# Requesting the MLP's weights in slices and reordering the opening of an attention-plus-MLP kernel

## The chip, the core and the metric

The kernel runs on one core of a Trainium2 chip. The metric is the device time of one execution in microseconds. PE is TensorE, ACT ScalarE, DVE VectorE, POOL GpSimd and SP SyncE, which here issues nearly all DMAs.

## What is computed

```
xn  = layernorm(x)                                    # x: 2048 x 640
q, k, v = split(xn @ wqkv)                            # 32 heads of 20
att = softmax(q @ k^T / sqrt(20)) @ v                 # per head
y   = layernorm(xn)
h   = gelu(y @ w1 + b1)                               # 640 -> 1536
out = x + att @ wo + (h @ w2 + b2)                    # 1536 -> 640
```

Inputs and the output are float32.

## The kernel before

The products are done in float16 pairs: a float32 number is scaled by a power of two and split into a high and a low half, and three products (high x high, high x low, low x high) stand for one. The power of two of each weight is found on the chip. ACT squares the weight and sums along the row (`Square` with `accum_out`), which gives a column per slice in a tile `acc`. `pow2` (L102) adds up the partitions with a product of `ones` and `acc` on PE (L111), adds up the columns on DVE (L112) and makes the power of two in five small DVE steps. `scale_of` (L416) calls it and leaves the scale `s_q`, `s_k` or `s_v` and, for q and k, the factor `qks`.

The program's first part runs over four chunks of 512 rows. Its order on each engine is the order in which it is written. For a chunk, rows are normalized (`norm_a` takes statistics and the root, `norm_b` refines it by a Newton step on DVE and scales the rows, `norm_c` refines the second layernorm's factor and stores it to `rscr`, a transfer of 512 pieces of four bytes), turned (`transp`, or in chunk 0 the transposes at L502 and L504) into `xnt`, and stored to `xscr` for the MLP. Then come five tiles `tt` of q and k: `qk` (30 products), `qk_out` (ACT makes the high half, DVE the low half in the buffer `hl`, of which there are two; two DMAs store it to `qkscr`), and `qk_sq` (squares for the lengths of the heads). Then come four tiles of v (`vproj`, `vproj_out`).

Chunk 0 is the opening. `load_x(0)` and the five slices of wqkv's q part are requested first, then its k part. `load_x(1)` reuses the tiles of x's first block and so waits for the transposes that read them; wqkv's v part, `xscr`, `bscr`, `b1t` and `rscr` follow in the same SP queue, and behind them the stores of the first q/k tile. `warm` issues products without a use, 37 at the start and 5 ahead of the first real ones. The tile `mxp` of `pow2` and the tile `pt4` of the fifth column of transposes share one PSUM buffer (`psM`), so that the transposes to `pt4` begin when DVE has read `mxp`. The q, k and v parts of wqkv are kept, until they are split, in the space of the MLP's weights: q and v in `w1t`, k in `w2t`.

The MLP's weights W1 (640 x 1536) and W2 (1536 x 640) are requested in chunk 0, each by one DMA: W2 behind tile 1 (L540), W1 in tile 4 (L548). `weights()` (L456) is a generator of small steps: six squares of W2 (two of its twelve row blocks each), its scale, five squares of W1 (a row block each), its scale, and then the splits. `some(n)` takes n of its steps, from the v tiles of chunk 0 on.

After chunk 3 the attention begins, with the MLP's and the output's products filled in between; the change doesn't touch that part.

Each DMA of SP's queue also waits until the DMA eight before it has landed, because the DMAs use eight semaphores in turn.

Of the kernel before, what the change touches and what calls it, by code (L numbers as in the profile page):

```python
# [7 lines left out]
F32 = mybir.dt.float32  # L8
# [3 lines left out]
AF = mybir.ActivationFunctionType  # L12
ALU = mybir.AluOpType
AX = mybir.AxisListType
PSUM = bass.MemoryType.PSUM
DRAM = bass.MemoryType.DRAM
P = 128
# [25 lines left out]
def mha_mlp_kernel(tc, x, wqkv, wo, w1, b1, w2, b2, out):  # L43
# [4 lines left out]
    with (  # L48
# [53 lines left out]
        def pow2(acc, tag):  # L102

            lo = keep.tile([P, 1], F32, name=f"lo_{tag}")
            hi = keep.tile([P, 1], F32, name=f"hi_{tag}")
            if tag in ("q", "k"):
                pt = psM.tile([P, 512], F32, tag="m", name="mxp")
            else:
                pt = psS.tile([P, 2, 512], F32, tag="s", name="mxp")[:, 0, :]
            n = acc.shape[1]  # L110
            nc.tensor.matmul(pt[:, :n], ones, acc, start=True, stop=True)  # L111
            nc.vector.tensor_reduce(lo, pt[:, :n], AX.X, ALU.add)  # L112
            nc.vector.tensor_scalar(lo, lo, 2.0**-100, 2.0**120, ALU.max, ALU.min)

            nc.vector.tensor_scalar(lo.bitcast(I32), lo.bitcast(I32), 0x7F000000, 1,
                                    ALU.bitwise_and, ALU.logical_shift_right)
            nc.vector.tensor_scalar(lo, lo, 2.0**64, None, ALU.mult)
            exponents(lo, hi)
            return lo, hi
# [42 lines left out]
        with tc.tile_pool(name="pa", bufs=2) as pa, tc.tile_pool(name="pa1", bufs=1) as pa1, tc.manual_schedule():  # L162
# [65 lines left out]
                nc.vector.tensor_scalar(t, t, -0.5 * by, 1.5 * by, ALU.mult, ALU.add)  # L228
                nc.vector.tensor_mul(dst, dst, t)

            def norm_a(c):

                xt = xts[c]
                st = pa.tile([P, 4, 2, 6], F32, tag="st", name="st")
                mv = pa.tile([P, 4, 2], F32, tag="mv", name="mv")
                ve = pa.tile([P, 4], F32, tag="ve", name="ve")
                r = pa.tile([P, 4], F32, tag="r", name="r")
                r2 = pa.tile([P, 4], F32, tag="r2", name="r2")
                for j in range(4):
                    for i in range(2):  # L240
                        nc.vector.bn_stats(st[:, j, i, :], xt[j][:, i * 320 : (i + 1) * 320])
                    nc.vector.bn_aggr(mv[:, j, :], st[:, j])
                nc.vector.tensor_scalar(ve, mv[:, :, 1], EPS, None, ALU.add)
                if c == 0:
                    nc.scalar.activation(r, ve, AF.Sqrt)
                    nc.vector.reciprocal(r, r)
                else:
                    nc.gpsimd.tensor_tensor(r, ve, nhalf, ALU.pow)
                rs[c] = mv, ve, r, r2
# [164 lines left out]
            def sums(tag, ws):  # L414
                accs[tag] = squares(ws, junk)
# [40 lines left out]
            def weights():  # L456

                for i in range(KF // 2):
                    if i == 0:
                        accs["2"] = sm.tile([P, 8], F32, tag="acc2", name="acc2", bufs=1)[:, : KF // 2]  # L460
                    nc.scalar.activation(junk[:, : 2 * D].rearrange("p (a b) -> p a b", a=2),
                                         w2t[:, 2 * i : 2 * i + 2, :], AF.Square, accum_out=accs["2"][:, i : i + 1])
                    yield
                scale_of("2")
                yield
                for k in range(KD):
                    if k == 0:
                        accs["1"] = sm.tile([P, 8], F32, tag="acc1", name="acc1", bufs=1)[:, :KD]
                    nc.scalar.activation(junk[:, :F], w1t[:, k, :], AF.Square, accum_out=accs["1"][:, k : k + 1])
                    yield  # L470
                scale_of("1")
                yield
                factors()
                yield
                for k in range(KF):
                    split(pa, w2t[:, k, :], w2v[:, k, 0], w2v[:, k, 1], scales["2"], D)
                    yield
                for k in range(KD):
                    for q in range(3):
                        split(pa, w1t[:, k, q * 512 : (q + 1) * 512], w1v[:, k, q, 0], w1v[:, k, q, 1], scales["1"], 512)  # L480
                        yield

            slices = weights()

            def some(n):
# [2 lines left out]


            warm(37)  # L490
            norm_a(0)
            sums("q", [stage["q"][:, k] for k in range(KD)])
            norm_b(0)
            xnts[0] = pa.tile([P, KD, 2, 512], F16, tag="xnt", name="xnt0")
            pts = [psS.tile([P, 2, 512], F32, tag="s", name="pt") for _ in range(2)]
            pt = [pts[0][:, 0], pts[0][:, 1], pts[1][:, 0], pts[1][:, 1]]
            for j in range(4):
                if j == 3:
                    scale_of("q")
                    pt.append(psM.tile([P, 512], F32, tag="m", name="pt4"))  # L500
                for k in range(KD - 1):
                    nc.tensor.transpose(pt[k][:, j * P : (j + 1) * P], xts[0][j][:, k * P : (k + 1) * P], ident)  # L502
            for j in range(4):
                nc.tensor.transpose(pt[4][:, j * P : (j + 1) * P], xts[0][j][:, 4 * P :], ident)  # L504
            warm(5)

            for k in range(KD):
                nc.scalar.activation(xnts[0][:, k, 0, :], pt[k], AF.Copy)
# [6 lines left out]
            for c in range(4):  # L515
                nxt = c + 1 if c < 3 else None
                for tt in range(5):
                    if c == 0 and tt == 1:
                        norm_b2(0)
                        norm_c(0)  # L520

                        nc.scalar.activation(junk[:, :1], ones[:, :1], AF.Exp)
                        ps = qk(0, 1, lambda: scale_of("k"))
                        hl = qk_out(0, 0, first)
                        split_qkv("q", c0=4 * P)
                        split_qkv("k")
                    else:
                        ps = qk(c, tt)
                    if tt == 3:
                        lengths(4)  # L530

                    if c == 0:
                        if tt == 0:
                            split_qkv("q", c0=2 * P, c1=4 * P)
                            sums("k", [stage["k"][:, 0:3], stage["k"][:, 3:]])
                            first = ps
                            continue
                        elif tt == 1:
                            qk_sq(0, 0, hl)
                            nc.sync.dma_start(w2t, w2.rearrange("(k p) n -> p k n", p=P))  # L540
                        elif tt == 2:
                            sums("v", [stage["v"][:, 0:3], stage["v"][:, 3:]])
                            norm_a(1)
                        elif tt == 3:
                            scale_of("v")
                            split_qkv("v")
                        elif tt == 4:
                            nc.sync.dma_start(w1t, w1.rearrange("(k p) n -> p k n", p=P))  # L548
                    else:

                        step = tt - (c == 1)
                        if nxt and 0 <= step < 3:
                            (norm_a, norm_b, norm_c)[step](nxt)
                            some(1)
                        else:
                            some(2)
                    qk_out(c, tt, ps)
                    if nxt and c > 0 and tt >= 2:
                        for j in ((0,), (1, 2), (3,))[tt - 2]:
                            turn(nxt, j)  # L560
                    if c == 3 and tt == 2:
                        early = [load_features(mc) for mc in range(2)]
                if c == 1:
                    load_x(3)
                if c == 3:
                    stack = load_stack(0, 0)
                    for _ in range(6):
                        next(stack)
                for j in range(4):
                    ps = vproj(c, j)  # L570
                    if j == (0 if c == 3 else 1):
                        lengths(10)
                    if c == 0:
                        if j < 2:
                            (norm_b, norm_c)[j](1)

                        pts = []
                        for k in ((), (0,), (2, 4), ())[j]:
                            transp(1, k, pts)
                        for t in pts:  # L580
                            transp_out(*t)
                    if j == 0 and c == 3:
                        shifts()
                        for _ in stack:
                            pass
                    some(2 if c < 3 else 1)
                    vproj_out(c, j, ps)
                if c == 0:
                    load_x(2)
            some(99)  # L590
# [630 lines left out]
```

## Time and profile before

| | us |
|---|---|
| median of 3 runs | 1363.1 (1362.19 to 1364.39) |
| profiled execution, its time | 1364.71 |
| its span | 1363.0 |
| PE busy in the span | 1335.1 (98%) |
| ACT busy | 1129.6 (83%) |
| DVE busy | 1060.5 (78%) |
| granted clock, mean | 0.998 |

Times in the views are counted from the start of the profiled execution's span; its time is 1.7 us more than its span. A row of a timeline has the start, the length, the engine, the line, the operation, what is written and read, and in brackets how long the engine was idle before it and who ended that.

### The profile page before, as it was taken

What the parts mean: (1) busy time and instruction counts of PE and PEld (TensorE: products, weight loads), DVE (VectorE), ACT (ScalarE), POOL (GpSimd) and SP (SyncE); (2) the same over time, 40 slices, a digit from 0 to 9 for tenths busy, and PEclk for the clock granted to TensorE, in tenths of its full rate; (3) what the DMA queues carried; (4) which work ended last, traced back from release to release, by engine and by line L of the source; (5) the groups of instructions that cost most, each with busy time, mean ns of one, the idle gap of its engine ahead of it and who ended that gap; (6) DMA issues with size and microseconds to landing.
All of it is one profiled execution on the core that took longest, in us unless ns stands there. A gap on an engine that the chain in (4) does not pass through costs nothing.

```text
span 1363.0 us, 29029 instructions
## 1 busy us (share of the span) xinstructions
PE 1335.1 (98%) x11651; PEld 591.6 (43%) x11651; DVE 1060.5 (78%) x1436; ACT 1129.6 (83%) x1305; POOL 30.2 (2%) x74
## 2 busy tenths in 40 slices
PE   9999999999999999999999999999999999999998
PEld 6545545443334334433433343434433333333465
DVE  6658835998779897978797789897879898888732
ACT  6654525999999999999999999999999999999700
POOL 2000000000000000000000000000000000000000
PEclk9999999999999999999999999999999999999999
DMA  9868731111113221212321141223032223244275
GB/s 269 270 157 154 146 101 57 34 52 43 48 58 94 62 83 60 52 50 84 93 71 51 37 109 48 86 62 86 19 87 85 70 81 86 59 135 118 88 233 175
DMA packets 103073, 127.94 MB, mean 94 GB/s; under 512 B 27516, under 2 KB 69568, under 8 KB 102932
## 3 DMA queue, kind: packets, MB, share of 16 engines
q1 hardware_dynamic: 99864, 119.60, 31.2%
q0 software_dynamic: 2304, 5.24, 2.4%
q8 instruction: 93, 1.52, 0.5%
q10 hardware_dynamic: 764, 1.18, 0.3%
q14 instruction: 48, 0.39, 0.1%
HBM read 80.50 MB, written 42.51 MB: 90 GB/s over the span
## 4 chain that ended last, share of the span: by engine, by line
PE 79%; DVE 9%; ACT 7%; issue 3%; DMA 2%; ACTq 0%; SPq 0%; DVEq 0%
PE o L711 26%; PE s L680 17%; PE py L945 11%; PE pu L913 9%; PE qkp L322 8%; PE vp L395 5%; ACT p L682 4%; PE z L1024 4%; DVE low L694 3%; DMA oa<-ev 1%; DVE u L849 1%; DMA qkscr<-qkhl 1%; DVE u L850 1%; DVE w L853 1%; DVE w L854 1%
## 5 line engine op out<-in xcount | busy, mean ns | idle before, releaser
L682 ACT ACTIVATE p<-s 128x1024 f32<-128x1024 f32 x1024 | 972.3, 1041 | 43.4 <-PE s L680 37.0
L694 DVE TENSOR_TENSOR low<-p 128x1024 f16<-128x1024 f32 x512 | 610.7, 1219 | 159.9 <-ACT p L682 159.7
L711 PE MATMUL o<-p,vfull 128*32 128x512 bf16 (+1 forms) x4096 | 430.8, 493 | 0.0
L680 PE MATMUL s<-qs,ks 61*128 61x512 f16 x2048 | 316.5, 382 | 7.4 <-ACT p L682 6.5
L680 PEld LDWEIGHTS <-ks 61*128 61x128 f16 x2048 | 63.7, 94 | 293.6 <-issue 291.3
L913 PE MATMUL pu<-xm,w1t 128*128 128x256 f16 x1440 | 179.3, 274 | 1.4 <-DVE u L849 1.4
L945 PE MATMUL py<-w2t,hT 128*128 128x320 f16 x1152 | 178.5, 300 | 1.5 <-DVE u L849 1.5
L913 PEld LDWEIGHTS <-w1t 128*128 128x128 f16 x1440 | 130.5, 98 | 68.8 <-issue 55.1
L945 PEld LDWEIGHTS <-hT 128*128 128x128 f16 x1152 | 102.4, 98 | 88.6 <-issue 54.3
L322 PE MATMUL qkp<-xnt,wv 128*128 128x512 f16 x600 | 132.7, 383 | 2.3 <-DVE qkhl L338 2.1
L711 PEld LDWEIGHTS <-vfull 128*32 128x32 f16 x3072 | 60.8, 95 | 139.8 <-issue 108.5
L711 PE MATMUL o<-low,vfull 128*32 128x512 f16 x1024 | 104.0, 378 | 4.3 <-DVE low L694 4.3
L322 PEld LDWEIGHTS <-wv 128*128 128x128 f16 x600 | 58.7, 99 | 73.2 <-issue 2.6
L711 PEld LDWEIGHTS o<-p,vfull 128*32 128x32 f32 x2048 | 62.6, 108 | 51.3
L337 ACT ACTIVATE qkhl<-qkp,qks 128x1024 f16<-128x1024 f32 (+1 forms) x24 | 23.2, 968 | 66.5 <-PE qkp L322 43.3
L1024 PE MATMUL z<-w1t,ot 128*128 128x320 f16 x480 | 66.7, 300 | 1.8 <-DVE oa L837 1.8
L395 PE MATMUL vp<-wv,xnt 128*128 128x320 f16 x480 | 66.7, 299 | 0.0
L338 DVE SCALAR_TENSOR_TENSOR qkhl<-qkp,qks,qkhl 128x1024 f16<-128x1024 f32 (+1 forms) x24 | 26.5, 1105 | 45.3 <-ACT qkhl L337 44.5
L1024 PEld LDWEIGHTS <-ot 128*128 128x128 f16 x480 | 46.3, 98 | 23.1 <-issue 2.9
L395 PEld LDWEIGHTS <-xnt 128*128 128x128 f16 x480 | 46.7, 98 | 18.7
L983 DVE SCALAR_TENSOR_TENSOR acc<-z,sc,acc 128x320 f32<-128x320 f32 x32 | 17.5, 550 | 43.2 <-PE z L1024 39.9
L732 ACT ACTIVATE ev<-o 128x512 f32<-128x512 f32 x64 | 39.2, 612 | 4.2 <-PE o L711 4.1
(179 smaller groups left out, 666.7 us busy)
## 6 DMA issues: line engine op xcount, KB each, us to landing
qkscr<-qkhl SPq DMA_DIRECT2D x40, 256.0 KB
opart<-ev SPq DMA_DIRECT2D x124, 80.0 KB
ks<-qkscr SPq DMA_DIRECT2D x120, 80.0 KB
qs<-qkscr SPq DMA_DIRECT2D x192, 40.0 KB
oa<-opart SPq DMA_DIRECT2D x32, 240.0 KB
xt<-in_A_x_dram SPq DMA_DIRECT2D x16, 320.0 KB
xscr<-xnt SPq DMA_DIRECT2D x4, 1280.0 KB
xm<-xscr SPq DMA_DIRECT2D x8, 640.0 KB
```

What stands on the lines that cost most here:

```text
L322: nc.tensor.matmul(ps[:, i, :], wv[:, k, q, a, mm * P : (mm + 1) * P], xnts[c][:, k, b, :], start=(k + n == 0), stop=(k == KD - 1 and n == 2))
L337: nc.scalar.activation(hl[:, 0, i0:i1], ps[:, i0:i1], AF.Copy, scale=a)
L338: nc.vector.scalar_tensor_tensor(hl[:, 1, i0:i1], ps[:, i0:i1], a, hl[:, 0, i0:i1], ALU.mult, ALU.subtract)
L395: nc.tensor.matmul(ps[:, hf, :320], xnts[c][:, k, a, j * P : (j + 1) * P], wv[:, k, 2, b, hf * 320 : (hf + 1) * 320], start=(n == 0), stop ...
L680: nc.tensor.matmul(ps[:, a, :], ks[64 * a : 64 * a + 61, kb * P : (kb + 1) * P], qs[64 * a : 64 * a + 61, cc * 512 : (cc + 1) * 512], star ...
L682: nc.scalar.activation(pt, ps, AF.Exp, scale=QS)
L694: nc.vector.tensor_sub(low, pt, upper(pt))
L711: nc.tensor.matmul(pv.o[32 * q : 32 * q + 32, :], src[:, v0 - PAD * (1 - q % 2) :][:, :32], t, start=q not in pv.begun, stop=last, skip_gr ...
L732: nc.scalar.activation(evs[g, hf][:, cc], pv.o, AF.Copy)
L913: nc.tensor.matmul(ps[:, i], w1v[:, k, (f + i) // 4, a, fo_ : fo_ + P], xnt[:, k, b, :], start=(n == 0), stop=(n == 3 * KD - 1))
L945: nc.tensor.matmul(ps[:, :320], hTs[mc][:, f, a, j * P : (j + 1) * P], w2v[:, f, b, hf * 320 : (hf + 1) * 320], start=(n == 0), stop=(n == ...
L1024: nc.tensor.matmul(ps[:, :320], ot[:, k, a, j * P : (j + 1) * P], wov[:, k, b, h * 320 : (h + 1) * 320], start=(n == 0), stop=(n == 3 * KD ...
```

## The change

The two DMAs for the MLP's weights become eleven: six for W2 (two row blocks each), five for W1 (one row block each). A generator `requests()` issues them, and `ask(n)` takes n: 1, 2, 2 and 1 behind `qk_out` of tiles 1 to 4 of chunk 0, then 2, 1, 1 and 1 behind its four v tiles.

In the opening, the square of q's first slice stands ahead of the `Sqrt` on ACT, the other four behind it. All sixteen transposes to the first four columns come ahead of `scale_of("q")`, where the last four stood behind it. The columns of `acc` are added up in PSUM, by one product for each column, and DVE's reduction is left out; this holds wherever `pow2` is called. Three products without use instead of five stand ahead of the first real ones.

```diff
             n = acc.shape[1]
-            nc.tensor.matmul(pt[:, :n], ones, acc, start=True, stop=True)
-            nc.vector.tensor_reduce(lo, pt[:, :n], AX.X, ALU.add)
-            nc.vector.tensor_scalar(lo, lo, 2.0**-100, 2.0**120, ALU.max, ALU.min)
+            for i in range(n):
+                nc.tensor.matmul(pt[:, :1], ones, acc[:, i : i + 1], start=(i == 0), stop=(i == n - 1))
+            nc.vector.tensor_scalar(lo, pt[:, :1], 2.0**-100, 2.0**120, ALU.max, ALU.min)
...
-            def norm_a(c):
+            def norm_a(c, between=None):
...
                 if c == 0:
+                    between()
                     nc.scalar.activation(r, ve, AF.Sqrt)
...
+            def requests():
+
+                for i in range(KF // 2):
+                    nc.sync.dma_start(w2t[:, 2 * i : 2 * i + 2], w2r[:, 2 * i : 2 * i + 2])
+                    yield
+                for k in range(KD):
+                    nc.sync.dma_start(w1t[:, k], w1r[:, k])
+                    yield
+
+            w2r, w1r = (w.rearrange("(k p) n -> p k n", p=P) for w in (w2, w1))
+            asked = requests()
+
+            def ask(n):
+                for _ in range(n):
+                    next(asked, None)
...
             warm(37)
-            norm_a(0)
-            sums("q", [stage["q"][:, k] for k in range(KD)])
+            accs["q"] = sm.tile([P, 8], F32, tag="acc", name="acc")[:, :KD]
+
+            def square_q(ks):
+                for k in ks:
+                    nc.scalar.activation(junk[:, :D], stage["q"][:, k], AF.Square, accum_out=accs["q"][:, k : k + 1])
+
+            norm_a(0, lambda: square_q((0,)))
+            square_q(range(1, KD))
             norm_b(0)
...
             for j in range(4):
-                if j == 3:
-                    scale_of("q")
-                    pt.append(psM.tile([P, 512], F32, tag="m", name="pt4"))
                 for k in range(KD - 1):
                     nc.tensor.transpose(pt[k][:, j * P : (j + 1) * P], xts[0][j][:, k * P : (k + 1) * P], ident)
+            scale_of("q")
+            pt.append(psM.tile([P, 512], F32, tag="m", name="pt4"))
             for j in range(4):
                 nc.tensor.transpose(pt[4][:, j * P : (j + 1) * P], xts[0][j][:, 4 * P :], ident)
-            warm(5)
+            warm(3)
...
                         elif tt == 1:
                             qk_sq(0, 0, hl)
-                            nc.sync.dma_start(w2t, w2.rearrange("(k p) n -> p k n", p=P))
...
-                        elif tt == 4:
-                            nc.sync.dma_start(w1t, w1.rearrange("(k p) n -> p k n", p=P))
...
                     qk_out(c, tt, ps)
+
+                    ask((0, 1, 2, 2, 1)[tt] if c == 0 else 0)
...
                     vproj_out(c, j, ps)
+                    if c == 0:
+                        ask(2 if j == 0 else 1)
```

## The prediction

> **What bounds the kernel now.** I read the page first. PE is busy 98% of the span and the chain of waits is 79% PE, so only time that PE loses counts. Of the groups of instructions, none that the change touches is large; all of it lies before 80 us. There I read the timeline engine by engine. PE, whole rows, then what holds it:
>
> ```profile
> 11.75 1.61 PE L502 MATMUL pt<-ident,xt 128*128 128x128 f32 x12 [0.17 <-DVE xt L255]
> 14.17 0.39 PE L111 MATMUL mxp<-acc,ones 128*128 128x5 f32 x2 [0.81 <-ACT junk L95]
> 14.41 0.63 PE L502 MATMUL pt<-ident,xt 128*128 128x128 f32 x4
> 14.88 0.60 PE L504 MATMUL pt<-ident,xt 128*128 128x128 f32 x4
> 15.32 1.28 PE L220 MATMUL warm<-ones 128*128 128x128 f32 x10
> 16.43 10.53 PE L322 MATMUL qkp<-xnt,wv 128*128 128x512 f16 x48
> ...
> 42.95 0.38 PE L111 MATMUL mxp<-acc,ones 128*128 128x2 f32 x2
> 45.47 8.34 PE L322 MATMUL qkp<-xnt,wv 128*128 128x512 f16 x30 [2.14 <-DVE qkhl L338]
> ```
>
> Each row is start, length, engine, line; the bracket is idle time before it. Real products begin at 16.43. From there PE stops once, for 2.14 us before 45.47, and otherwise runs on past 220 us (its only other gap there is 0.20 us at 73.21). So there are two prices: when 16.43 comes, and the stall at 43.33.
>
> The chain of waits names the stall's cause, and the busy time by stretch shows what surrounds it (columns: stretch, length, PE, PEld, DVE, ACT, POOL busy, clock, DMA share, GB/s):
>
> ```profile
> 31.22 10.78 DMA qkscr<-qkhl
> 42.00 0.02 issue
> 42.02 0.04 ACTq L337
> 42.06 0.38 issue
> 42.44 0.69 ACT qkhl L337
> ```
> ```profile
> 32.50:38.00 5.50, 5.50 (x28) 2.46 (x26) 5.04 (x10) 5.47 (x6) 0.00 (x0) 1.00 0.87 19
> 42.80:46.20 3.40, 1.26 (x22) 0.72 (x11) 2.15 (x7) 2.07 (x3) 0.00 (x0) 1.00 1.00 375
> 46.20:49.60 3.40, 3.40 (x10) 1.21 (x9) 2.47 (x5) 3.14 (x5) 0.00 (x0) 0.50 1.03 403
> 1305.70:1309.10 3.40, 1.61 (x13) 0.94 (x12) 2.67 (x3) 0.00 (x0) 0.00 (x0) 1.00 0.02 8
> ```
>
> The copy-out of the third q/k tile (tt 2) reuses the first tile's buffer, and must wait for that tile's two stores, 256 KB each, which take 10.78 us. From 32.5 to 38 the DMA engines are 87% busy and move 19 GB/s: this follows `rscr`'s store of 512 four-byte pieces, and the same collapse follows the next `rscr` stores at 73 and 106 us. W2's 3.84 MB is requested at 34.99, behind these stores, and its packets start only at 38.85, when the collapse is over. So the stall is `rscr`'s doing, not W2's. After the stall the clock is 0.50 for 3.4 us; the 30 matmuls take 8.34 instead of 30 x 0.215 = 6.45 us, some 1.8 us more.
>
> The opening's ACT rows, and the one table load with work on both sides:
>
> ```profile
> 9.75 0.21 ACT L245 ACTIVATE r<-ve 128x4 f32<-128x4 f32 x1 [7.64 <-DVE ve L243]
> 9.86 0.72 ACT L95 ACTIVATE junk<-w1t 128x640 bf16<-128x640 f32 x1
> 10.48 0.19 ACT L95 ACTIVATION_READ_ACCUMULATOR junk<-w1t 128x1 f32 x1
> ...
> 25.59 0.19 ACT L95 ACTIVATION_READ_ACCUMULATOR junk<-w2t 128x1 f32 x1
> 25.86 1.28 ACT L522 ACT_TABLE_LOAD   x1
> 27.15 0.20 ACT L522 ACTIVATE junk<-ones 128x1 bf16<-128x1 f32 x1
> ```
>
> **Square before root.** Before, one table load at 0.82 serves Sqrt and the squares. In the changed program's order ACT has a load, the square, a second load, then the Sqrt. Q's first slice arrives at 9.02 (the arrivals of its transfer), so the square runs 9.06 to 9.88 (0.62 + 0.19). The load then costs 27.15 - 25.78 = 1.37, and the root starts at 11.25 instead of 9.75: +1.50. The square was to be free in ACT's idle time; its cover ends with the load. DVE's Newton step and row scaling follow the root directly, so the last normalized tile comes at 14.67 instead of 13.17, and its four transposes (0.11 each) end at 15.17. The other four squares, 0.86 apart from 11.36, end at 14.80 and are no longer last. The Trainium skill, page "ScalarE: Activation LUTs", section "What ACT_TABLE_LOAD costs", gives 1283 ns plus a drain of about 1380 ns for a switch; by that the total below would be 1.3 higher, 1366.3. The rows show the 1.28 and no drain beside it.
>
> **Column sums.** One product of five columns (two passes, 0.13 + 0.25) becomes five of one column, ten passes, and DVE's reduction (0.20 with its wait) goes. No row shows such a chain. The nearest:
>
> ```profile
> L826 PE MATMUL rb<-lt,sel x32: 231/232/251, 1298.0 to 1300.3; 64*80 64x64 f32 x32
> ```
>
> 32 passes start within 2.24 us, 0.072 each, with 80 columns of weights; at 128 columns in proportion 0.115. Bounds are 0.072 (weights do not matter) and 0.13 (the start-to-start of `mxp`'s two passes). I take 0.115, because these weights have 128 columns: the last pass starts at 15.18 + 9 x 0.115 = 16.22 and ends 0.25 later. DVE reads at 16.49, where before its second step stood at 14.79: the q scale is +1.70 (1.3 to 1.85).
>
> **First products, warm-up, transfers.** The q scale releases ACT's first split (15.73, now 17.43), that ends 0.51 later, and products start at 17.95 to 18.05 instead of 16.43: +1.6. Three warm-ups instead of five end at 17.9 behind the last transposes and cost nothing; two more would end at 18.3. The fifth column's transposes now wait for DVE's read: 16.79 instead of 14.88. SP issues x's second block (15.29) only when they are through, so at 17.2: +1.9, with wqkv's v part, `xscr`, `rscr` and the first q/k stores behind it on one queue. The DMA engines are busy without a break from there (1.02 between 20 and 30 us), so the first stores land 1.9 later, at 43.9, and tt 4's products start at 47.4. PE's stall becomes 2.4 instead of 2.1. If the queue has 0.3 of slack, it is +1.6.
>
> **Eleven slices.** 11 issues of about 0.43 instead of 2 on SP: 4 us more on an engine that stood idle 7.3 us at 48.40 and 4.8 at 59.56; free, and without that cover the q/k stores queued behind would be as late. The stores of tt 1 now pass W2, so ACT's wait of 4.43 before 54.59 goes. That frees nothing on PE: tt 3's bank was free at 57.02, and its user, the second v product, came at 57.7. Next in line is v's split (done 51.4, used from 53.65); it moves with tt 2. The tt 2 wait of 2.82 stays, since nothing that goes ahead of the first stores is changed. W1's last slices come behind `xscr`, near 80 us; ACT waited 6.0 us for W1 until 79.16 before, and PE ran on. Cost: nothing.
>
> **Sum.** The profiled execution took 1364.71; 1364.71 + 1.9 = 1366.6. The median of the runs is 1.6 lower, 1363.1, and gives 1365.0. The half-clock stretch will come in some runs and not in others, since the same stall lies elsewhere in the clock's 3.41 us grid (without it, 1.8 less); I take it as often as before.
>
> **Rivals.**
> *The stall closes.* If W2's reads slowed the tail of the first stores (packets of both overlap from 38.85 to 41.3), tt 2's copies would be held by DVE's statistics of x's second block (until 40.9), tt 4 could start at 43.2 + 1.6, and 2.14 and the 1.8 go: 1363.1 + 1.6 - 3.9 = 1360.8, between 1359.6 and 1362. For it: that overlap, and arrivals 2.1 us after the small packets against 0.35 at 57.4. Against it: the collapse starts 2.5 us before W2's request. Chance 0.20.
> *The clock falls in the opening* (slower). PE idles from 11.57 to 13.24, then has transposes and one-column passes until 17.2. A window of 3.41 us laid there is about half busy. 1.26 of 3.40 lost the clock, 1.61 of 3.40 kept it; the point that decides is between. It costs one window at half rate: 1365.0 + 1.7 = 1366.7. By the skill's page "TensorE: Matmul & The Clock Gate", section "Part 4: PE-mode transpose", transposes do not count as PE-busy in the same way; by that the window would be nearly empty. The trace speaks against it: 12.1 to 15.5 was almost only transposes, and the clock stayed 1.00. Chance 0.16.
> *The switch of tables drains ACT* for as long again as it loads, 1.3: 1366.3. Against it stands the row at 25.86. Chance 0.06.
> That the square moves ahead without a load is excluded by the program's order.
>
> **Numbers.** 0.2%, 2.7 us, is about what a measurement of this kernel can tell from no change: faster is under 1360.4, slower over 1365.8. The forecast has 0.58, spread 1364.0 to 1366.2, of which 0.07 lies over 1365.8. Slower: 0.07 + 0.16 + 0.06 = 0.29. Faster: 0.09, the lower part of the first rival. Same: 0.62. The range 1360.8 to 1367.2 leaves out 0.10 below and little above.
>
> **What would show it.** Two ACT table loads before 12 us and the root near 11.25; ten `mxp` passes ending near 16.5; first products near 18.0; x's second block issued near 17.2; ACT still waiting for `qkscr` until about 44.3, PE idle some 2.4 us; no wait for `qkscr` at tt 3. I am wrong if the root comes before 10.2, or if PE does not stop before tt 4.

## The result and the profile after

| | before | changed |
|---|---|---|
| median of 14 runs each, us | 1362.8 (1361.05 to 1366.33) | 1365.2 (1364.15 to 1368.24) |
| ratio, with its 95% interval | | 1.0019 (1.0011 to 1.0027) |
| profiled execution, us (span) | 1364.71 (1363.0) | 1366.54 (1364.8) |

The changed kernel is slower by 0.19%, 2.4 us by the medians. The forecast was 1365.0. It was right in the total and in the opening. What it said of the stall ahead of tile 4 and of the slices was wrong, and it left the column sums outside the opening out; these errors cancelled. The rest of this document is about that.

PE's timeline of the changed kernel, the rows that answer to those of before:

```profile
12.49 2.14 PE L522 MATMUL pt<-ident,xt 128*128 128x128 f32 x16 [0.58 <-DVE xt L256]
14.46 1.17 PE L112 MATMUL mxp<-acc,ones 128*128 128x1 f32 x10
15.89 0.66 PE L526 MATMUL pt<-ident,xt 128*128 128x128 f32 x4 [0.25 <-DVE lo_q L113]
16.38 0.83 PE L220 MATMUL warm<-ones 128*128 128x128 f32 x6
17.18 10.67 PE L323 MATMUL qkp<-xnt,wv 128*128 128x512 f16 x48
...
44.49 6.63 PE L323 MATMUL qkp<-xnt,wv 128*128 128x512 f16 x30
...
70.04 1.40 PE L112 MATMUL mxp<-acc,ones 128*128 128x1 f32 x12
...
97.63 1.28 PE L112 MATMUL mxp<-acc,ones 128*128 128x1 f32 x10
```

The same two sums (W2's and W1's) on PE before:

```profile
72.73 0.28 PE L111 MATMUL mxp<-acc,ones 128*128 128x6 f32 x2
99.54 0.39 PE L111 MATMUL mxp<-acc,ones 128*128 128x5 f32 x2
```

Four things are to be seen. The ten passes of q's column sum and the waits around them are as forecast. The row at 44.49 has no bracket: PE no longer stops ahead of tile 4, where it had stopped 2.14 us and the forecast had 2.4. Its 30 products take 6.63 us instead of 8.34, so that the half-rate stretch is gone there. And two rows stand at the bottom of the first view that the forecast never looked for: the sums of W2's six and W1's five columns, now 1.40 and 1.28 us on a PE that has no idle time there. Before, these took two passes each, 0.28 and 0.39.

ACT's timeline of the changed kernel, in the opening and at tile 2:

```profile
8.34 0.74 ACT L512 ACTIVATE junk<-w1t 128x640 bf16<-128x640 f32 x1 [6.24 <-DMA w1t<-in_A_wqkv_dram]
8.98 0.19 ACT L512 ACTIVATION_READ_ACCUMULATOR junk<-w1t 128x1 f32 x1
9.19 1.28 ACT L246 ACT_TABLE_LOAD   x1
10.48 0.21 ACT L246 ACTIVATE r<-ve 128x4 f32<-128x4 f32 x1
...
41.31 0.69 ACT L338 ACTIVATE qkhl<-qkp,qks 128x512 f16<-128x512 f32 x1 [0.80 <-DMA qkscr<-qkhl]
```

The second table load is there, and the root follows it. The rows' statistics (`ve`) were ready at 8.75 in this execution, 0.96 earlier than in the profile of before, because the input transfers landed earlier. So the root is 1.73 later than its inputs, where before it was 0.03. At tile 2 ACT still waits for the first stores, but 0.80 us instead of 2.82. At tile 3 it no longer waits for them.

The busy time by stretch (columns as in the prediction):

```profile
32.50:38.00 5.50, 5.50 (x28) 2.47 (x26) 5.08 (x8) 5.47 (x7) 0.00 (x0) 1.00 0.87 50
46.20:49.60 3.40, 3.40 (x17) 1.57 (x16) 3.13 (x4) 3.40 (x6) 0.00 (x0) 1.00 0.89 289
1309.85:1313.25 3.40, 3.40 (x15) 1.91 (x14) 2.41 (x4) 0.00 (x0) 0.00 (x0) 0.50 0.71 208
```

The collapse of the DMA rate behind `rscr`'s store is still there (87% busy, 50 GB/s). The half clock has moved: it is not at 46.2 but at 1309.85, behind a PE stop of 2.13 us in the last products. (In the profile of before, the stop at that place was 1.79 and the clock stayed.)

PE's operations can be laid side by side. The changed kernel's lead (minus) or lag (plus) at each is then a ledger of the 1.8 us between the two profiled spans:

| where | lag after it, us | what it is |
|---|---|---|
| first product | +0.75 | opening +1.71 behind `ve`, and `ve` 0.96 earlier |
| 40 us | +1.07 | k's column sum, 0.22; the first products run 0.14 longer |
| tile 4, 44.5 | -0.98 | the stall of 2.14 is gone |
| 49.8 | -2.68 | no half clock there |
| 73 | -1.91 | W2's column sum, 0.97, less a gap of 0.20 |
| 99.8 | -1.02 | W1's column sum, 0.89 |
| 1238 | -0.07 | wo's column sum, 0.9 |
| 1309 | +0.31 | longer PE gaps in the last stage |
| 1311 | +1.95 | half clock at 1309.85 |
| end | +1.84 | |

### The profile page after: what moved, and what is told of

The parts are those of the page before. It is cut to its first block, busy times and chain, and to the rows that moved or that the text cites. A ratio compares the mean times of both kernels' runs of the same rounds, so it can differ in the third digit from the quotient of the medians.

```text
span 1364.8 us, 29104 instructions
## 1 busy us (share of the span) xinstructions
PE 1338.9 (98%) x11685; PEld 596.4 (44%) x11685; DVE 1060.2 (78%) x1429; ACT 1130.7 (83%) x1306; POOL 30.2 (2%) x74
## 4 chain that ended last, share of the span: by engine, by line
PE 80%; DVE 8%; ACT 5%; DMA 2%; issue 2%; SPq 1%; ACTq 0%; DVEq 0%
PE o L734 26%; PE s L703 16%; PE py L968 11%; PE qkp L323 10%; PE pu L936 9%; PE vp L396 5%; ACT p L705 4%; PE z L1047 4%; DVE low L717 3%; DMA oa<-ev 1%; DVE u L872 1%; DVE u L873 1%; DMA ks<-qkscr 1%; DVE w L876 1%; DVE w L877 1%
## 5 line engine op out<-in xcount | busy, mean ns | idle before, releaser
L339 DVE SCALAR_TENSOR_TENSOR qkhl<-qkp,qks,qkhl 128x1024 f16<-128x1024 f32 (+1 forms) x24 | 26.5, 1106 | 39.4 <-ACT qkhl L338 39.2
```

What stands on the lines that cost most here:

```text
L339: nc.vector.scalar_tensor_tensor(hl[:, 1, i0:i1], ps[:, i0:i1], a, hl[:, 0, i0:i1], ALU.mult, ALU.subtract)
```

## The experiments

All were timed in five rounds beside the kernel before on the same chip. That kernel's median was 1363.5 us beside the first four, 1364.0 beside the next four, and 1364.1 beside the last four. Each ratio is against it. The medians are over 11 runs, for e10 to e12 over 5.

| run | what it has | median, us | ratio (95%) |
|---|---|---|---|
| e1 | before, with the slices | 1361.7 | 0.9986 (0.9977 to 0.9995) |
| e2 | before, with column sums on PE | 1364.9 | 1.0005 (0.9996 to 1.0014) |
| e3 | before, with the new opening (old sums) | 1363.7 | 1.0001 (0.9992 to 1.0010) |
| e4 | changed, old sums, root's table first | 1362.0 | 0.9987 (0.9978 to 0.9996) |
| e5 | changed kernel again | 1366.1 | 1.0015 (1.0006 to 1.0024) |
| e6 | changed, old sums | 1362.4 | 0.9989 (0.9980 to 0.9998) |
| e7 | before, W2 whole behind tile 1's stores | 1362.7 | 0.9995 (0.9986 to 1.0004) |
| e8 | before, `rscr` store later | 1360.4 | 0.9975 (0.9966 to 0.9984) |
| e9 | changed, root's table first | 1364.5 | 1.0007 (0.9998 to 1.0016) |
| e10 | changed, `rscr` store later | 1372.2 | 1.0060 (1.0046 to 1.0074) |
| e11 | before, slices and `rscr` store later | 1368.6 | 1.0035 (1.0021 to 1.0048) |
| e12 | e4 with `rscr` store later | 1370.2 | 1.0043 (1.0029 to 1.0057) |

### The three parts alone

**e1, the slices alone.** The hunks of `requests`, `ask` and the two removed DMAs, and nothing else:

```diff
                             qk_sq(0, 0, hl)
-                            nc.sync.dma_start(w2t, w2.rearrange("(k p) n -> p k n", p=P))
...
-                        elif tt == 4:
-                            nc.sync.dma_start(w1t, w1.rearrange("(k p) n -> p k n", p=P))
...
                     qk_out(c, tt, ps)
+                    ask((0, 1, 2, 2, 1)[tt] if c == 0 else 0)
...
                     vproj_out(c, j, ps)
+                    if c == 0:
+                        ask(2 if j == 0 else 1)
```

> The kernel before with the eleven slices alone; opening and pow2 as before. Theory A (W2 behind the first stores lengthens them): PE's stall before tt 4 shrinks from 2.1 to under 0.5 us, and with the half-clock stretch behind it the median falls by 2 to 4 us. Theory B (the collapse after rscr's store has a length of its own that varies from run to run, and the shorter one after the change was not the slices' doing): the stall stays between 1.5 and 2.5 us and the median within 0.7 us of before.

Measured: 0.9986, a gain of 1.7 us by the medians, and the interval doesn't reach 1. That is between what the two theories said. PE's row at tile 4 in e1:

```profile
42.98 6.65 PE L322 MATMUL qkp<-xnt,wv 128*128 128x512 f16 x30 [0.21 <-DVE lo_v L112]
```

The stall is 0.21 here, and tile 3's copies on ACT start without a wait. The forecast's "That frees nothing on PE" is refuted by the gain. What the gain consists of is the matter of e3, e7 and e8.

**e2, the column sums alone.** Only the hunk of `pow2`:

```diff
-            nc.tensor.matmul(pt[:, :n], ones, acc, start=True, stop=True)
-            nc.vector.tensor_reduce(lo, pt[:, :n], AX.X, ALU.add)
+            for i in range(n):
+                nc.tensor.matmul(pt[:, :1], ones, acc[:, i : i + 1], start=(i == 0), stop=(i == n - 1))
```

> The kernel before with pow2's sum by one product per column, alone. Theory A (the column sums cost PE where nothing hides them: at the q scale, and at the scales of W2, W1 and wo, which the prediction left out): each chain of 10 or 12 passes is some 0.9 us longer, so about +0.7 by 16 us, +0.8 at 73, +0.9 at 100 and +0.9 at 1238 us, together +3 to +3.6. Theory B (what was lost after 71 us comes from W1's later slices or from the run itself): +0.5 to +1, all of it in the opening.

Measured: 1.0005 (0.9996 to 1.0014). By the rows, each sum over five or six columns is longer by 0.9 us, at 69.13, 96.71 and 1235.96 in e2 (Theory A's places), and PE has no idle time that takes it: from chunk 1's first product to its tile 4, across W1's sum, 27.46 us pass where it was 26.57. In the opening the sum costs nothing, because in the old order PE stood idle for 0.81 us ahead of it, waiting for the square of the fifth slice. The passes for the first four columns now fall into that time, from 13.18 to 14.13, and only the fifth column's two come behind that square, as two did before. The first product comes 6.69 behind the root in both. The profiled execution of e2 had no stall ahead of tile 4 (no bracket in its row) although W2 is asked for whole:

```profile
43.58 6.63 PE L322 MATMUL qkp<-xnt,wv 128*128 128x512 f16 x30
```

The median of e2 is nearer to that of before than 2.7 us of rows would make it: 0.7 by the ratio, 1.4 by the medians. Whether the stall is also shorter in e2's other runs can't be seen, and this part stays open.

**e3, the opening alone.** The square ahead of the root, the order of the transposes and three products without use, with the old `pow2` and the two whole requests:

```diff
                 if c == 0:
+                    between()
                     nc.scalar.activation(r, ve, AF.Sqrt)
...
-                if j == 3:
-                    scale_of("q")
-                    pt.append(psM.tile([P, 512], F32, tag="m", name="pt4"))
...
+            scale_of("q")
+            pt.append(psM.tile([P, 512], F32, tag="m", name="pt4"))
...
-            warm(5)
+            warm(3)
```

> The kernel before with the square ahead of the root, scale_of behind all sixteen transposes and three warm-up products, alone; whole requests and the one-product sum as before. Theory A: two table loads, the root 0.75 to 1.5 later according to when q's first slice arrives, and without the column sums the first products 0 to 0.8 us later than 16.43; median 0 to +1. Theory B (the order of the opening is worth what the square saves): first products 0.7 earlier, median -0.7.

Measured: 1.0001, no difference that shows. The second table load is at 9.71 and the root at 11.01, 1.59 behind `ve`. From the root to the first product it is only 6.00 us instead of 6.69. So the order gains 0.7 and the load loses 1.6. The timeline of e3, ACT and PE rows, shows a limit that before did not bind:

```profile
53.89 1.11 ACT L338 ACTIVATE qkhl<-qkp,qks 128x1024 f16<-128x1024 f32 x1 [4.92 <-DMA qkscr<-qkhl]
56.38 4.25 PE L396 MATMUL vp<-wv,xnt 128*128 128x320 f16 x30 [1.37 <-DVE qkhl L339]
62.55 4.24 PE L396 MATMUL vp<-wv,xnt 128*128 128x320 f16 x30 [0.45 <-DVE vfull L408]
```

In this execution the stall ahead of tile 4 was 0.24. PE arrived earlier at the v products, and there it ran into tile 3's copies, which had waited 4.92 us for stores queued behind W2's 3.9 MB. This is the wait that the forecast called free, because in the profile of before PE came 0.7 us later than the bank. In that profile PE had lost 3.9 us ahead of it. The wait doesn't bind each time that the stall is short: in e2, where W2 had landed at 49.4 instead of 52.5, ACT waited 2.48 at tile 3 and PE not at all.

### Which cost is which

**e5, the changed kernel again**, beside the next runs, with nothing edited.

> The changed kernel once more, on the chip of the next three, so that its parts can be set against it. All theories: 1.5 to 3 us over before. Its profile: root 1.5 to 1.7 behind the variance it needs, first products 6.70 behind the root, chains of column sums of 1.2 to 1.4 us near 70, 98 and 1237 us, no ACT wait for qkscr at tt 3.

Measured: 1.0015. The root is 1.60 behind `ve`, and the first product is 6.69 behind the root. PE's stop ahead of tile 4 is 0.36 in this execution, with ACT waiting 1.45 for the first stores.

**e6, the changed kernel with the old sums.**

```diff
-            for i in range(n):
-                nc.tensor.matmul(pt[:, :1], ones, acc[:, i : i + 1], start=(i == 0), stop=(i == n - 1))
+            nc.tensor.matmul(pt[:, :n], ones, acc, start=True, stop=True)
+            nc.vector.tensor_reduce(lo, pt[:, :n], AX.X, ALU.add)
```

> The changed kernel with pow2 as before (one product, then the reduction); slices, square ahead of the root, three warm-ups as changed. Theory A (the sums cost 0.7 in the opening, where they now stand behind the transposes, 0.2 at v and 0.85 each at W2, W1 and wo): 3.4 us under the changed kernel, 0.5 to 1.5 under before. Theory B (they cost what they cost alone, 1.4): 1.4 under the changed kernel, 0.5 to 1 over before.

Measured: 1362.4 against 1366.1 of e5 on the same chip, 3.6 us. The column sums turn a kernel that is faster than before into one that is slower; the intervals of the two ratios don't touch. The rows give 0.7 in the opening (6.69 against 6.00 from root to first product) and three times 0.9 at W2, W1 and wo, 3.4 in all, which is Theory A's sum.

**e9, the changed kernel with the root's table first.** One more instruction, a `Sqrt` of one column at the start:

```diff
             warm(37)
+            nc.scalar.activation(junk[:, :1], ones[:, :1], AF.Sqrt)
             accs["q"] = sm.tile([P, 8], F32, tag="acc", name="acc")[:, :KD]
```

> The changed kernel (slices, square ahead of the root, sums by columns on PE) with one more instruction: a one-column Sqrt ahead of all else on ACT, so that the table that holds both Sqrt and Square is loaded once, at the start. Theory A: the second table load alone holds the root, by 1.5 to 1.7 us. The root comes 0.2 behind the square (about 1.7 behind the last statistics before, about 0.4 now), the first real products at 16.3 to 16.6 instead of 17.8, and the time falls by 1.0 to 1.6 against the changed kernel: 1364.4 to 1365.0 where that has 1366.0. Theory B: the opening is given back before tt 4, because the first stores land when the collapse behind the rscr store ends: PE idles 1 us or more before tt 4, and the time is that of the changed kernel within 0.5.

Measured: 1364.5, with a ratio of 1.0007 where the changed kernel has 1.0015 to 1.0019. ACT's timeline of e9:

```profile
0.82 1.28 ACT L508 ACT_TABLE_LOAD   x1 [0.82 <-PEq L1232]
...
9.27 0.19 ACT L513 ACTIVATION_READ_ACCUMULATOR junk<-w1t 128x1 f32 x1
9.37 0.19 ACT L246 ACTIVATE r<-ve 128x4 f32<-128x4 f32 x1
```

One load, in the time in which ACT waits for data anyway, now serves both functions, and the root is 0.27 behind `ve`. The first product comes at 16.16. By the rows the load costs 1.3 to 1.5 us; the medians agree (1.1 by the ratios, 1.6 by the differences to before), but the intervals overlap. The profiled execution had a stall of 1.32 ahead of tile 4, so Theory B's mechanism exists. The medians don't show that it takes the gain back, but with overlapping intervals they can't exclude it.

**e4, the same with the old sums.** The edits of e9 and e6 together:

```diff
+            nc.scalar.activation(junk[:, :1], ones[:, :1], AF.Sqrt)
             accs["q"] = sm.tile([P, 8], F32, tag="acc", name="acc")[:, :KD]
...
+            nc.tensor.matmul(pt[:, :n], ones, acc, start=True, stop=True)
+            nc.vector.tensor_reduce(lo, pt[:, :n], AX.X, ALU.add)
```

> The changed kernel with pow2 as before (one product, then the reduction) and with a Sqrt of one column ahead of the first square, so that one table load at 0.8 us serves both. Theory A: no second table load, root at its time of before (9.0 to 9.8), four squares left behind it, first products 0.3 to 0.8 us earlier than 16.43, no stall before tt 4: 3 to 5 us under before. Theory B (the stall is not the slices' doing): 0.3 to 0.8 under before.

Measured: 0.9987, where e1 has 0.9986 and e6 0.9989. That is 1.5 us under before by the medians, 1.8 by the ratio, and between what the two theories said. Here the faster opening (5.99 from the root to the first product, at 15.63) brought nothing that can be told from no gain. The profile shows PE standing still 1.11 us ahead of tile 4 instead of 0.21 in e1: the time gained at the start is waited out where the first stores land. Why the load shows in the time with the column sums (e5 to e9) and not without (e6 to e4) isn't settled. The four intervals would allow the same 0.8 us in both.

### What holds PE ahead of tile 4

The forecast said that the slices can't touch the stall, since nothing ahead of the first stores changes. The stall was nevertheless gone. Either W2's whole transfer had slowed the stores' tail (the rival), or the collapse differs from run to run.

**e7, W2 whole, but requested behind tile 1's stores:**

```diff
                             qk_sq(0, 0, hl)
-                            nc.sync.dma_start(w2t, w2.rearrange("(k p) n -> p k n", p=P))
...
                     qk_out(c, tt, ps)
+                    if c == 0 and tt == 1:
+                        nc.sync.dma_start(w2t, w2.rearrange("(k p) n -> p k n", p=P))
```

> The kernel before with W2's one DMA issued behind the stores of q/k tile 1 instead of ahead of them; W1 and all else as before. Theory A (what the slices gain is that tile 1's stores no longer stand behind W2, so that tile 3's copies and with them the second v product need not wait): no ACT wait for qkscr at tt 3, and 1 to 2 us under before, like the slices. Theory B (slicing itself matters, since now the stores of tiles 2 and 3 stand behind W2's whole 3.84 MB): the wait moves to tile 4's copies, up to 55 us, and less than 0.7 us is gained.

Measured: 0.9995 (0.9986 to 1.0004). There is no stall ahead of tile 4 in this execution, and tile 3's copies don't wait; but tile 4's now do, 3.89 us, and a v product waits 0.76 at 60.26. A whole request has only changed the stores that it blocks. Behind the slices, which have stores between them, ACT waits for no store at tiles 3 and 4 in any of the six profiles that have them and the `rscr` store in its old place. By these rows that is what e1 has over e7; the intervals of the two ratios overlap.

**e8, chunk 0's `rscr` store behind tile 4's stores**, W2 and W1 as before:

```diff
                 newton(r2, ve, "b")
-                nc.sync.dma_start(rscr[c * 512 : (c + 1) * 512].rearrange("(j p) -> p j", p=P), r2)
+                if c > 0:
+                    store_r(c, r2)
+                else:
+                    late.append(r2)
...
                     qk_out(c, tt, ps)
+                    if c == 0 and tt == 4:
+                        store_r(0, late.pop())
```

> The kernel before with chunk 0's store to rscr issued behind the stores of tile 4 instead of ahead of the first stores; nothing else. Theory A (its 512 four-byte pieces cause the collapse of the writes behind it): the first stores arrive by 34, no packet of theirs takes over 2 us, ACT does not wait for them at tt 2, PE does not stop before tt 4, and the collapse shows behind the new place, near 60 us; 1 to 3 us under before, since W2 then still stands ahead of tile 1's stores. Theory B (the collapse comes from the stores themselves or from W2): the first stores still arrive near 40.

Measured: 0.9975 (0.9966 to 0.9984), 3.6 us under before and the fastest version of all, a little more than Theory A said. Its 11 runs lie within 1.5 us (1360.08 to 1361.58), the 11 runs of each of the kernels e1 to e7 and e9 within 2.2 to 5.3. The timelines of PE and ACT, and the busy time by stretch, in e8:

```profile
42.75 6.63 PE L330 MATMUL qkp<-xnt,wv 128*128 128x512 f16 x30
...
50.75 1.11 ACT L345 ACTIVATE qkhl<-qkp,qks 128x1024 f16<-128x1024 f32 x1 [2.99 <-DMA qkscr<-qkhl]
...
59.41 2.88 PE L403 MATMUL vp<-wv,xnt 128*128 128x320 f16 x20 [0.41 <-DVE vfull L415]
```
```profile
32.50:38.00 5.50, 5.50 (x28) 2.48 (x26) 5.04 (x9) 5.44 (x7) 0.00 (x0) 1.00 0.43 115
```

The first stores land at 31.3 and 32.0 instead of about 42, before W2 is even requested (34.54). So the collapse ahead of them is `rscr`'s doing, as the forecast said. In e8 it shows from 70 to 75 us (90% busy, 36 GB/s), where PE runs on.

Whether W2's reads lengthen the stores' tail can't be seen in e8, where the two don't overlap; e2 and e3 show it. There W2 is asked for whole, and its packets start at 36.21 and 37.44, 2.2 and 3.5 us before the second of the first stores lands. That store still lands 23.1 and 25.0 us after x's second block was requested, where the six profiles with slices have 24.8 to 26.5 and before has 26.7. So W2's overlap is not what makes the stores late: the rival's mechanism is refuted, though its outcome came. With the small pieces ahead of the first stores, the landing lay between 23.1 and 26.7 us in ten profiles, without any order between kernels with and without slices. The stall is what is left of that draw, and the narrow runs of e8 fit this. It was 2.14 in the one profile from which the forecast read it, and 0 to 1.32 in the nine later profiles of kernels with that store in its old place.

The gain of e8 is more than the stall. PE's stops between the first product and chunk 1 add up to 0.6 us in e8 and to 2.3 both in before (2.14 and 0.20) and in e3 (0.24, 1.37, 0.45 and 0.20): what isn't lost ahead of tile 4 can be lost at the v products. In the profile of before the half-rate stretch adds 1.7. What the 3.6 us of the medians consist of, beyond the stops, isn't located.

### Why the two gains don't add

What suggests itself is to have both, the slices and the later `rscr` store. **e11** is before with these two; **e10** is the changed kernel with the later store; **e12** is e4 with it. The edit is that of e8 in each.

> The kernel before with the eleven slices and the later rscr store, nothing else. Theory A: two separate limits, the collapse before tt 4 and W2's 3.84 MB ahead of tile 1's stores (0.41 us of PE's idle time before a v product with the later store alone), are both gone: PE has no stop over 0.25 us between the first product and 220 us, and the time is 0.3 to 0.8 under the later store alone, which took 1360.4 where the kernel before had 1364.0 (ratio 0.9975): ratio 0.997. Theory B: the slices add nothing once the collapse is out of the way: 0.9975 to 0.998.

> The changed kernel with one edit: chunk 0's rscr store is issued behind the stores of tile 4 instead of ahead of the first q/k stores. Theory A: the stall before tt 4 is 0 to 2 us from run to run in every kernel with that store ahead, and goes for good: the first stores land about 33, ACT doesn't wait for qkscr at tt 2, PE runs through tt 4, and the median falls by 0.4 to 1.5 against the changed kernel (1364.5 to 1365.6 where that has 1366.0) with a narrower spread. Theory B: in the changed kernel the late opening already covers the collapse, so the edit gains under 0.3, or the slices, which now share the engines with the late rscr store, are held by it and PE waits at the v tiles or in chunk 1 instead.

> The version that the runs point to: the slices, the later rscr store, the square of q's first slice ahead of the root with the root's table loaded at the start, the transposes in the changed order, and the sum over the columns of acc left on DVE as before. Theory A: against the slices with the later store alone the first real products come 0.5 to 0.7 earlier behind the root (6.0 instead of 6.7), nothing behind them waits, and the time is lower by as much: ratio 0.9965 against the kernel before, 1358.7 to 1359.3 where that has 1363.5. Theory B: DVE's copies and statistics around tt 4 (1.4 us of ACT's wait for DVE with the later store alone) become the limit, and the 0.6 is lost there: the same as the slices with the later store, within 0.2.

Measured: 1.0035, 1.0060 and 1.0043. All three are 4.5 to 8 us slower than before. The stall ahead of tile 4 is gone in each, and the first stores land at 30.5 to 33.4, as Theory A of e10 said; in the time every Theory A fell. Theory B of e10 had named the way (slices held by the late store, PE waiting in chunk 1); none had the size. In e11, PE's rows, ACT's, the busy time by stretch, and the chain of waits:

```profile
70.34 0.39 PE L111 MATMUL mxp<-acc,ones 128*128 128x6 f32 x2 [2.16 <-ACT junk L469]
102.20 5.10 PE L330 MATMUL qkp<-xnt,wv 128*128 128x512 f16 x15 [2.88 <-DVE qkhl L346]
...
68.92 1.27 ACT L469 ACTIVATE junk<-w2t 128x1280 bf16<-128x1280 f32 x1 [2.46 <-DMA w2t<-in_B_w_dram]
87.80 1.48 ACT L477 ACTIVATE junk<-w1t 128x1536 bf16<-128x1536 f32 x1 [4.54 <-DMA w1t<-in_B_w_dram]
```
```profile
60.00:65.00 5.00, 5.00 (x41) 3.99 (x40) 2.10 (x3) 4.28 (x7) 0.00 (x0) 1.00 0.98 52
```
```profile
67.24 20.48 DMA w1t<-in_B_w_dram
```

The late store comes at 52.8, chunk 1's own `rscr` store follows at 58.7, and the last slices of W2 and all of W1 stand among and behind them. From 60 to 65 us the DMA engines are 98% busy and move 52 GB/s. W2's last slice is there only for the square at 68.92, and PE waits 2.16 us for the column sum that needs it. W1's slices hold ACT's squares until 87.80, and chunk 1's copies stand behind them on ACT, down to a PE stop of 2.88 at 102.20. Half the clock follows twice, at 72.24 and 102.96. The two stops and the two half-rate stretches (1.7 us each) come to 8.4 us, and the profiled execution of e11 took 8.35 us longer than that of e1, which lacks only the later store. In e8, W2 had landed at 49.4 and W1 was requested ahead of both `rscr` stores: from 60 to 65 us its engines moved 401 GB/s. The collapse doesn't go away when the store is moved. It falls on what is behind the store.

## Why the prediction was right or wrong, point by point

- **Second table load.** Right. The root was 1.6 to 1.7 behind `ve` in each kernel with the square first and no earlier `Sqrt` (forecast +1.50), and 0.27 in e9. The load takes 1.28 and the root starts 0.01 after it. There is no drain: between the end of the accumulator read (9.17) and the load (9.19) lie 0.02 us, so the last rival (0.06) fell, and with it the 1380 ns of the Trainium skill's page "ScalarE: Activation LUTs", section "What ACT_TABLE_LOAD costs", for this place.
- **Column sums in the opening.** Right. The passes start 0.113 apart (0.115 was taken), the first product came 1.71 later behind `ve` (+1.6). That a pass of one column costs as much as this fits the Trainium skill, "TensorE: Matmul & The Clock Gate", section "LDWEIGHTS (loading the stationary operand)": a load of weights takes as long as it has columns, whatever its rows, by its rule an estimate of 107 ns for 128 columns.
- **The opening's delay reaches tile 4, and the stall stays at 2.4.** Wrong: the failed step is "so the first stores land 1.9 later, at 43.9", and with it "PE's stall becomes 2.4 instead of 2.1". They landed at 40.8 and 41.1, the second 24.8 us behind x's second block instead of 26.7, and the stall was 0. By the prediction's own sign ("or if PE does not stop before tt 4") this part fell. The step took the length of one collapse in one execution for a constant.
- **Eleven slices: nothing.** Wrong by 1.7 us (e1, by the medians). The step "That frees nothing on PE" compared a bank free at 57.02 with a user at 57.7. That user stood behind the 3.9 us of stall and half clock. With the stall short, the same wait can bind (e3: 1.37 and 0.45; e8: 0.41; e2: not). That the slices' gain is this wait is argued from these rows; no run takes the wait away alone.
- **Column sums elsewhere.** Left out of the sum altogether, although the front section says that they change wherever `pow2` is called. The missing terms are 0.9 each at W2, W1 and wo, and some 0.2 at k and v: 2.9 us with no cover, on an engine that the forecast itself calls 98% busy.
- **The half clock "as often as before".** It came in the profiles of the changed kernel at 1309.85 and at 1301.88 (e5), not at 46. The rival that put one into the opening (0.16) did not come: the clock was 1.00 from 5.96 to 1309.85, through the transposes.
- **The sum.** +1.9 on the profile of 1364.71 gave 1366.6, and the profiled execution took 1366.54. The parts were +1.7 for the opening, -1.0 for inputs that came earlier in that execution, about +2.9 for sums that were left out, -3.8 for a stall and a half clock that were said to stay, and +2.0 for a longer stop and a half clock at the end. The outcome of the first rival, which had 0.20, came in the middle of the kernel, while the total stayed at the forecast. The total was right by cancellation, which is luck.

## What to carry to other kernels

When a helper is changed, count its calls over the whole program before working on the one call that the change was made for: here the other three cost more than the one. A stall read from a single profile is one draw, so its length has to come from several, and a wait called free must be checked again with the stalls ahead of it taken away. A store of many small pieces costs what stands behind it in the queue; moving it helps only if nothing urgent stands there, and the gain of moving it and the gain of splitting what follows need not add.

## What the runs showed of the hardware

- A store of 512 pieces of four bytes holds the writes behind it by some 6 to 9 us: the second of the first two 256 KB stores took 8.8 to 11.6 us from its request to its landing in the ten profiles with those pieces ahead of it, and 2.3 to 3.0 in the four without (e8, e10 to e12). The engines count as 87 to 98% busy meanwhile, at 19 to 52 GB/s. The Trainium skill, "DMA: Bandwidth & Descriptors", section "Specifications", says that transfers under 512 B are done by read-modify-write. These runs agree that such pieces are costly, but they don't show by which mechanism the later, large stores are held.
- In e11 two such stores came 5.9 us apart, and a slice of W1 requested behind them (0.79 MB) took 20.48 us.
- A half-rate stretch of 3.41 us (twice that in e12, at 99.5) comes behind a PE stop in some executions and not in others: it begins at 46, 72, 100, 102, 103, 1300, 1302, 1310 or 1315 us in different kernels, or nowhere but at the very end (e1, e3, e4, e6, e7, e8). At 46 in before and at 1310 in the changed kernel it costs half its length, 1.7 us, as much as the change's whole delay of the opening. Near 1300 in e2 and e5 it costs less, for there the PE stop that follows is 0.2 to 0.3 us, where the other profiles have 1.05 to 2.47.
